# A scatter in front of all others, and VectorE's turned squares behind the choice of the group in front

## The chip, the cores and the metric

The kernel runs on one core of one Trainium2 chip. The metric is the device time of one execution in microseconds (us), the median of several; lower is better. The profile shows one further execution of the same program.

## The reference

The input x has 8 batches of 3584 rows of 192 values. First comes a causal convolution over the rows: 7 taps for each of 8 heads of 24 columns, the taps being a softmax of `weight`. Each of the 28672 rows that come out is then sent to one of 8 experts:

```
logits = x @ w_gate + modality_bias[modality_id]
e_idx  = argmax(logits, axis=1)
gate_w = softmax(logits)[e_idx]
out[rows of e] = gate_w * (relu(x[rows of e] @ w1[e]) @ w2[e])
```

w1[e] is 192 x 1024 and w2[e] is 1024 x 192.

## The kernel before, in words

**Routing.** The rows are taken in tiles of 120 positions of one batch; four tiles are a quad, and a group has 1, 1, 2, 1, 1, 2 and then 4 quads (`QUADS_OF_GROUP`). Groups are numbered from 0 here, so the words "groups two to six" of the change mean numbers 1 to 5 (the code gives pins to numbers 1 to 4). For each group:

- SP (SyncE) loads the rows `x` (L317, L320), one load per quad.
- `convolve` (L336) multiplies them on PE (TensorE) by a band matrix (`cv`, L365 while a group has its x whole, else L349); ACT (ScalarE) or DVE (VectorE) copies the result to one of four buffers `y` (L368, L370).
- `turn` (L381) lets DVE transpose squares of 32 x 32 of `y` into `turned` (L385); `gate` (L399) multiplies them on PE by w_gate (`gt`, L405); `logits` (L410) turns the result back and adds the bias (`lt` L412, `lg` L415).
- `choose` (L419) finds the expert on DVE: `top`, `ex`, `rk`, `first`, `oh` (L441, a one where the expert is), `den`.
- `place` (L453) counts on PE how many rows go to each expert (`rp`, L463, L466) and makes on DVE the row number of each token (`carry`, `pos`, `row`, `idx` L487).
- `send` (L492) lets POOL (GpSimd) scatter each tile's rows to the DRAM buffer `routed_rows`, one indirect DMA per tile (`scatter`, L249, issued on L251). Before a group's scatters POOL writes the token numbers into `y` (L448).

**Experts.** Groups 0 to 3 (5 quads, 20 tiles) are chunk 0. `table` (L626) shares the rows of a chunk out to slots, each of one expert. A `Slot` (L725) loads the expert's weights by SP (`raw1` L736, L738; `raw2` L741) and `bring` (L745) loads the routed rows (L771). The first slot's rows go to `raw2` of the other buffer and are turned by PE (`tps`, L802 to L804); `first` (L828) and `second` (L845) are then the two products of the expert (`hps` L835, `po` L855 and L859), which run for the rest of the kernel, with the routing of the later groups between them.

**What sets the order.** Each engine works off its own list in order. A scheduler orders the lists while the program is built, by its own estimate of when each instruction is ready; `tc.issue_after(i)` puts an instruction behind `i` in that order. SP's list is a queue as well: while its first instruction waits, all behind it wait. The load of the first slot's rows waits until all 20 scatters of chunk 0 have landed:

```
for c, name in scatters if self.i < always else ():
    if c <= chunk:
        tc.add_manual_dep(ld, name, ...)
```

Group 7's x stands in a buffer of four loads, one per quad. A convolution product takes the x of eight tiles, so that the first products of group 7 want the first two of these loads.

Of the kernel before, what the change touches and what calls it, by code (L numbers as in the profile page):

```python
# [9 lines left out]
F32 = mybir.dt.float32  # L10
F32R = mybir.dt.float32r
BF16 = mybir.dt.bfloat16
I32 = mybir.dt.int32
AF = mybir.ActivationFunctionType
ALU = mybir.AluOpType
# [3 lines left out]
P = 128  # L19
# [30 lines left out]
def conv_then_routed_ffn(ctx, tc, x, weight, modality, w_gate, mod_bias, w1, w2, out):  # L50
    nc = tc.nc
    NB, S, D = x.shape
# [11 lines left out]
    OVER = 2  # L64
    Q = 32
    NK = D // Q
    W = D + OVER
# [9 lines left out]
    const = ctx.enter_context(tc.tile_pool(name="const", bufs=1))  # L77
# [11 lines left out]
    turns, state = {}, {}  # L89

    def ring(pool, n, shape, dtype, name, tag=None):

        tag = tag or name
        k = turns[tag] = turns.get(tag, -1) + 1
        return pool.tile(shape, dtype, name=name, tag=f"{tag}_{k % n}", bufs=1)
# [20 lines left out]
    ident = const.tile([P, P], F32, name="ident")  # L116
# [4 lines left out]
    def warm(n):  # L121

        for _ in range(n):
# [7 lines left out]
        out=tri, in_=ones, compare_op=ALU.is_gt, fill=0.0, base=0,  # L131
        pattern=[[1, MB]], channel_multiplier=-1,
# [6 lines left out]
                   base=0, channel_multiplier=0, allow_small_or_imprecise_dtypes=True)  # L139
# [59 lines left out]
    def make_modality():  # L199
        both = const.tile([MB, 2, E], F32, name="both")  # L200
        nc.scalar.dma_start(out=both.rearrange("p m e -> p (m e)"),
                            in_=mod_bias.rearrange("m e -> (m e)").partition_broadcast(MB))
        step = const.tile([MB, E], F32, name="step")
        nc.vector.tensor_tensor(out=step, in0=both[:, 1, :], in1=both[:, 0, :], op=ALU.subtract)
        room, ids, each = modality_rows
        low = room[0:each, 4 * MB:6 * MB].rearrange("p (q s) -> p q s", q=2)
        with tc.issue_after(state["line"]):
            nc.vector.tensor_copy(out=low, in_=ids.rearrange("p q (s two) -> p q s two", two=2)[:, :, ::-1, 0])
        mt_ps = ring(ps_t, 4, [MB, 2, each], F32, "mt_ps", "t")
        for q in range(2):  # L210
            nc.tensor.transpose(out=mt_ps[:, q], in_=low[:, q, :], identity=ident[0:each, 0:each])
        mt = const.tile([MB, NB, NSB], F32, name="mt")
        with tc.issue_after(state["wg"]):
            nc.vector.tensor_copy(out=mt.rearrange("p b s -> p (b s)"), in_=mt_ps.rearrange("p q r -> p (q r)"))
        return both[:, 0, :], step, mt
# [43 lines left out]
    def routed(chunk, ins):  # L259
# [3 lines left out]
        tc.add_to_no_dep_group(f"rows{chunk}", ins)  # L263
        scatters.append((chunk, ins.name))

    def make_bias(dst, n, ids):
        nb = ids.shape[1]
        nc.gpsimd.tensor_tensor(
            out=dst.rearrange("p (s b) e -> p s b e", s=n), in0=ids.rearrange("p b s -> p s b").unsqueeze(3).broadcast_to([MB, n, nb, E]),
            in1=step.unsqueeze(1).unsqueeze(1).broadcast_to([MB, n, nb, E]), op=ALU.mult)  # L270
        nc.gpsimd.tensor_tensor(out=dst, in0=dst, in1=start_row.unsqueeze(1).broadcast_to([MB, n * nb, E]), op=ALU.add)
# [5 lines left out]
    class Group:  # L277
# [103 lines left out]
        def turn(self, q):  # L381

            t0 = self.b0 + 4 * q % NB
            self.turned = ring(gp, 2, [P, NK, 4, Q], F32, "turned")
            nc.vector.transpose(out=self.turned.rearrange("p k t c -> p t k c"),  # L385
                                in_=self.ys[4 * q // NB][:, t0:t0 + 4, OVER:W].rearrange("p t (k c) -> p t k c", c=Q))

        def part_turned(self, q):

# [29 lines left out]
        def choose(self):  # L419

            n = self.tiles
            lg = self.lg

            def per_tile(ap):
                return ap.unsqueeze(2).broadcast_to([MB, n, E])

            top = rt.tile([MB, NT], F32, name="top")[:, 0:n]
            nc.vector.tensor_reduce(out=top, in_=lg, axis=AX.X, op=ALU.max)
            ex = rt.tile([MB, NT, E], F32, name="ex", bufs=1)[:, 0:n]
            nc.vector.tensor_tensor(out=ex, in0=lg, in1=per_tile(top), op=ALU.subtract)  # L430
            self.oh_and_none = rt.tile([MB, NT, E], BF16, name="oh")[:, 0:n + (self.g < SUMMED)]
            self.oh = self.oh_and_none[:, 0:n]
            if self.g < SUMMED:
                nc.vector.memset(self.oh_and_none[:, n], 0.0)
            rk = rt.tile([MB, NT, E], F32, name="rk", bufs=1)[:, 0:n]
            nc.vector.scalar_tensor_tensor(out=rk, in0=ex, scalar=0.0, in1=ramp.unsqueeze(1).broadcast_to([MB, n, E]),
                                           op0=ALU.is_equal, op1=ALU.mult)
            state["exp"] = nc.scalar.activation(out=lg, in_=ex, func=AF.Exp).ins
            first = rt.tile([MB, NT], F32, name="first")[:, 0:n]
            nc.vector.tensor_reduce(out=first, in_=rk, axis=AX.X, op=ALU.max)  # L440
            nc.vector.tensor_tensor(out=self.oh, in0=rk, in1=per_tile(first), op=ALU.is_equal)  # L441
            den = rt.tile([MB, NT], F32, name="den")[:, 0:n]
            nc.vector.tensor_reduce(out=den, in_=lg, axis=AX.X, op=ALU.add)
            nc.vector.tensor_scalar(out=den, in0=den, scalar1=1e-9, scalar2=None, op0=ALU.add)
            for i, y in enumerate(self.ys):
                nc.vector.reciprocal(out=y[0:MB, self.b0:self.b0 + self.nb, 0], in_=den[:, i * self.nb:(i + 1) * self.nb])
                with tc.issue_after(state["scatter"]) if "scatter" in state else nullcontext():
                    nc.gpsimd.iota(y.bitcast(I32)[0:MB, self.b0:self.b0 + self.nb, 1], pattern=[[S, self.nb]],  # L448
                                   base=self.b0 * S + (self.block + i) * MB - CUT + MB - 1,
                                   channel_multiplier=-1)  # L450
# [47 lines left out]
    FIRST = GROUPS_OF_CHUNK[0]  # L498
# [54 lines left out]
    def load_early(g):  # L553
        early.append(Group(g, chunk_of[g]))
        for q in range(early[-1].quads):
            early[-1].load(q, g >= CLEARED)
# [339 lines left out]
    for g in range(CLEARED):  # L896
        with tc.issue_after(state["band"]) if g >= BEFORE_BAND else nullcontext():
            load_early(g)
    start_row, step, mt = make_modality()
    init_tables()  # L900
    make_keep()
    first_bias = const.tile([MB, 6 * NB, E], F32, name="first_bias")
    make_bias(first_bias, 6, mt[:, :, 0:6])
    for y in y_bufs[1:]:
        clear(y)
# [176 lines left out]
```

## Time and profile before

| | us |
|---|---|
| median of 3 executions | 1239.13 (1236.37, 1239.13, 1240.28) |
| the profiled execution | 1235.66 |
| span of its instructions | 1233.9 |
| PE busy in it | 1212.0 (98%) |
| DVE busy | 964.4 (78%) |
| ACT busy | 721.0 (58%) |
| POOL busy | 526.6 (43%) |

The span runs from the first to the last instruction; 1.8 us of the execution lie around it. PE busy nearly all the time says that an end is moved only by what makes PE wait, by what PE has to do and by its clock. The waits lie in the first 65 us, where the routing of chunk 0 runs before the first expert can start; so the rows further down are nearly all from that stretch. Times in them are us from the start of the span.

### The profile page before, as it was taken

To read this page: it belongs to the slowest core of one execution; us is meant where nothing else is said; L and a number is where in the kernel's file an instruction comes from. 1 tells how busy PE (TensorE), PEld (TensorE's weight loads), DVE (VectorE), ACT (ScalarE), POOL (GpSimd) and SP (SyncE) were. 2 spreads that over 40 slices of the span, in tenths; PEclk is the share of its full clock that TensorE was granted. 3 is DMA by queue.
4 is the path that set the end of the run, shared out by engine and by line. 5 is a ranking of instruction groups with operands and counts; after the bars stand their busy time and mean duration, and the time that the engine had idled before them with its cause. 6 is when DMAs were issued, how large, how long until landed. Compare 5 with 4: busy or idle time off the path is not lost.

```text
span 1233.9 us, 28026 instructions
## 1 busy us (share of the span) xinstructions
PE 1212.0 (98%) x9244; PEld 1198.9 (97%) x9244; DVE 964.4 (78%) x2453; ACT 721.0 (58%) x1584; POOL 526.6 (43%) x549
## 2 busy tenths in 40 slices
PE   9899999999999999999999999999999999999996
PEld 7899999999999999999999999999999999999995
DVE  7787786888788888888878887777766766787894
ACT  2365565565666556666655665555555555566783
POOL 7756564636344343545435344344352122112221
PEclk9999999999999999999999999999999999999998
DMA  8897563345544354345432554233262344953271
GB/s 217 235 239 182 126 175 78 76 107 150 137 87 114 77 130 109 66 113 147 126 70 59 109 124 123 53 73 61 62 169 56 81 106 91 255 125 96 43 190 38
DMA packets 308448, 144.29 MB, mean 117 GB/s; under 512 B 222922, under 2 KB 294930, under 8 KB 308293
## 3 DMA queue, kind: packets, MB, share of 16 engines
q1 hardware_dynamic: 284574, 97.83, 36.8%
q0 software_dynamic: 22752, 44.54, 11.6%
q8 instruction: 74, 1.21, 0.4%
q14 instruction: 81, 0.66, 0.2%
q10 hardware_dynamic: 967, 0.03, 0.0%
HBM read 116.58 MB, written 51.82 MB: 136 GB/s over the span
## 4 chain that ended last, share of the span: by engine, by line
PE 85%; DVE 5%; DMA 4%; issue 2%; ACT 1%; POOL 1%; SPq 1%; POOLq 0%; DVEq 0%; ACTq 0%
PE hps L835 39%; PE po L855 25%; PE po L859 12%; PE gt L405 4%; PE cv L349 3%; PE cv L365 2%; DMA raw<-in_moe_w_dram 1%; DVE hl L839 1%; DMA xr<-in_x_dram 1%; DVE w1b L110 1%; DVE xl L110 1%; DMA routed_rows<-y,idx 1%; DVE w2b L110 1%; DMA near<-routed_rows 1%; ACT lowp L871 1%
## 5 line engine op out<-in xcount | busy, mean ns | idle before, releaser
L855 PE MATMUL po<-w2b,hh 128*128 128x384 f32 x1824 | 555.9, 355 | 0.0
L835 PE MATMUL hps<-sxh,w1b 128*128 128x256 f32 x1824 | 481.8, 287 | 3.1 <-DVE hl L839 1.7
L839 DVE SCALAR_TENSOR_TENSOR hl<-hps,hh 128x512 fp32r<-128x512 f32 x456 | 311.6, 685 | 198.0 <-ACT hh L838 195.6
L838 ACT ACTIVATE hh<-hps 128x512 fp32r<-128x512 f32 x456 | 272.8, 598 | 327.7 <-PE hps L835 322.2
L859 PE MATMUL po<-w2b,hl 128*128 128x192 f32 x1824 | 443.0, 253 | 0.0
L874 POOL DMA_INDIRECT out_dram<-o,tags x228 | 236.3, 1036 | 382.0 <-DVE o L873 323.3
L251 POOL DMA_INDIRECT routed_rows<-y,idx x240 | 260.8, 1087 | 304.1 <-DVE hl L839 145.7
L835 PE MATMUL hps<-sxs,w1b 128*128 128x256 f32 x1824 | 363.2, 281 | 0.4 <-DVE sxs L822 0.4
L835 PEld LDWEIGHTS hps<-sxh,w1b 128*128 128x128 f32 x1824 | 344.5, 189 | 8.4 <-DVE hl L839 7.8
L859 PEld LDWEIGHTS po<-w2b,hl 128*128 128x128 f32 x1824 | 345.7, 190 | 0.0
L855 PEld LDWEIGHTS po<-w2b,hh 128*128 128x128 f32 x1824 | 344.1, 189 | 0.5 <-DVE o L873 0.2
L835 PEld LDWEIGHTS hps<-sxs,w1b 128*128 128x128 f32 x1824 | 279.8, 189 | 0.7 <-issue 0.7
L835 PE MATMUL hps<-sxl,w1b 128*128 128x256 f32 x912 | 256.0, 281 | 0.0
L835 PEld LDWEIGHTS hps<-sxl,w1b 128*128 128x128 f32 x912 | 172.8, 189 | 0.0
L110 DVE TENSOR_TENSOR w1b<-raw,w1b 128x512 fp32r<-128x512 f32 x152 | 101.4, 675 | 5.9 <-ACT w1b L108 5.5
L871 ACT ACTIVATE lowp<-po,tags 128x192 f32<-128x192 f32 x228 | 83.6, 417 | 31.1 <-PE po L855 29.7
L108 ACT CAST w1b<-raw 128x512 fp32r<-128x512 f32 x152 | 92.7, 620 | 2.0 <-DMA raw<-in_moe_w_dram 1.3
L110 DVE TENSOR_TENSOR w2b<-raw,w2b 128x384 fp32r<-128x384 f32 x152 | 80.7, 541 | 8.2 <-ACT w2b L108 7.8
L873 DVE SCALAR_TENSOR_TENSOR o<-po,tags,lowp 128x192 f32<-128x192 f32 x228 | 84.6, 411 | 2.2 <-ACT lowp L871 2.2
L820 ACT CAST sxs<-tp 64x128 fp32r<-64x128 f32 x224 | 66.7, 298 | 30.7 <-DVE tp L795 28.0
L108 ACT CAST w2b<-raw 128x384 fp32r<-128x384 f32 x152 | 75.9, 512 | 1.0
L822 DVE TENSOR_TENSOR sxs<-tp,sxs 64x128 fp32r<-64x128 f32 x224 | 64.8, 289 | 8.6
(158 smaller groups left out, 962.8 us busy)
## 6 DMA issues: line engine op xcount, KB each, us to landing
raw<-in_moe_w_dram SPq DMA_DIRECT2D x38, 768.0 KB
raw<-in_moe_w_dram SPq DMA_DIRECT2D x38, 512.0 KB
raw<-in_moe_w_dram SPq DMA_DIRECT2D x76, 256.0 KB
near<-routed_rows SPq DMA_DIRECT2D x208, 64.0 KB
xr<-in_x_dram SPq DMA_DIRECT2D x32, 384.0 KB
x<-in_x_dram SPq DMA_DIRECT2D x26, 384.0 KB
routed_rows<-filler SPq DMA_DIRECT2D x9, 776.0 KB
far<-routed_rows SPq DMA_DIRECT2D x208, 32.0 KB
```

Source lines behind the costliest of these rows:

```text
L108: nc.scalar.copy(out=hi, in_=raw)
L110: return nc.vector.tensor_tensor(out=lo, in0=raw, in1=f(hi), op=ALU.subtract).ins
L251: state["scatter"] = nc.gpsimd.indirect_dma_start(out=scr, out_offset=bass.IndirectOffsetOnAxis(ap=idx, axis=0), in_=src, in_offset=None,).ins
L820: nc.scalar.copy(out=hi, in_=raw)
L835: nc.tensor.matmul(hps[:, u, :], wa[:, c, fs], mv[z], start=n == 0, stop=n == len(terms) - 1)
L838: nc.scalar.activation(out=hh, in_=hps, func=AF.Relu)
L839: hl_ins = nc.vector.scalar_tensor_tensor(out=hl, in0=hps, scalar=0.0, in1=f(hh), op0=ALU.max, op1=ALU.subtract)
L855: nc.tensor.matmul(po, hh[:, u, js], wb[:, c, :], start=c == 0, stop=c == NF - 1, skip_group_check=True)
L859: nc.tensor.matmul(po[:, 0:D], hl[:, u, js], wb[:, c, 0:D], start=False, stop=False, skip_group_check=True)
L871: nc.scalar.activation(out=lowp, in_=po[:, D:2 * D], func=AF.Copy, scale=gate)
L873: turn_behind(nc.vector.scalar_tensor_tensor(out=o, in0=po[:, 0:D], scalar=gate, in1=lowp, op0=ALU.mult, op1=ALU.add))
L874: st = nc.gpsimd.indirect_dma_start(out=out, out_offset=bass.IndirectOffsetOnAxis(ap=tag.bitcast(I32)[:, j, 1:2], axis=0), in_=o, in_offse ...
```

## The change

Three edits. (1) A new function `scatter_once` issues, after the bands and the gate are made, one indirect DMA of 128 rows of two values from `ident` into a DRAM buffer of its own, `first_rows`, which nobody reads. (2) `choose` keeps its `oh` instruction in `state["oh"]`. (3) In `turn`, for groups 1 to 4 the first quad's transposition is put behind the `oh` of the group in front, and the second quad's (only group 2 has one) behind the `idx` of the group in front. Pins are of order alone and add no wait.

```diff
+    def scatter_once():
+        at = const.tile([P, 1], I32, name="at")
+        nc.gpsimd.iota(at, pattern=[[0, 1]], base=0, channel_multiplier=1)
+        first = nc.dram_tensor("first_rows", (P, OVER), F32, kind="Internal").ap()
+        nc.gpsimd.indirect_dma_start(out=first, out_offset=bass.IndirectOffsetOnAxis(ap=at, axis=0),
+                                     in_=ident[:, 0:OVER], in_offset=None)
...
             self.turned = ring(gp, 2, [P, NK, 4, Q], F32, "turned")
-            nc.vector.transpose(out=self.turned.rearrange("p k t c -> p t k c"),
-                                in_=self.ys[4 * q // NB][:, t0:t0 + 4, OVER:W].rearrange("p t (k c) -> p t k c", c=Q))
+            pin = state["idx" if q else "oh"] if 0 < self.g <= FIRST else None
+            with tc.issue_after(pin) if pin else nullcontext():
+                nc.vector.transpose(out=self.turned.rearrange("p k t c -> p t k c"),
+                                    in_=self.ys[4 * q // NB][:, t0:t0 + 4, OVER:W].rearrange("p t (k c) -> p t k c", c=Q))
...
-            nc.vector.tensor_tensor(out=self.oh, in0=rk, in1=per_tile(first), op=ALU.is_equal)
+            state["oh"] = nc.vector.tensor_tensor(out=self.oh, in0=rk, in1=per_tile(first), op=ALU.is_equal).ins
...
             load_early(g)
+    scatter_once()
     start_row, step, mt = make_modality()
```

The scheduler then orders other instructions anew as well. After the first expert products of slot 0 the lists of all engines are again the same; before them they differ in places. The line numbers of the changed kernel are 7 to 10 higher.

**VectorE, from the copy of group 0's convolution to its `idx` (L487, in the changed kernel L496).** `y_182` is the buffer of groups 0 and 1. Before:

```order
L385 STREAM_TRANSPOSE turned<-y_182 128x4x6x32
L370 COPY y_182<-cv 120x2x4x24
L412 STREAM_TRANSPOSE lt<-gt 128x128
L415 TENSOR_TENSOR lg<-lt,first_bias 120x32
L428 TENSOR_REDUCE top<-lg 120x4
L385 STREAM_TRANSPOSE turned<-y_182 128x4x6x32
L430 TENSOR_TENSOR ex<-lg,top 120x32
L436 SCALAR_TENSOR_TENSOR rk<-ex,ramp 120x32
L440 TENSOR_REDUCE first<-rk 120x4
L443 TENSOR_REDUCE den<-lg 120x4
L441 TENSOR_TENSOR oh<-rk,first 120x32
```

Now:

```order
L421 STREAM_TRANSPOSE lt<-gt 128x128
L424 TENSOR_TENSOR lg<-lt,first_bias 120x32
L437 TENSOR_REDUCE top<-lg 120x4
L439 TENSOR_TENSOR ex<-lg,top 120x32
L445 SCALAR_TENSOR_TENSOR rk<-ex,ramp 120x32
L449 TENSOR_REDUCE first<-rk 120x4
L452 TENSOR_REDUCE den<-lg 120x4
L450 TENSOR_TENSOR oh<-rk,first 120x32
L394 STREAM_TRANSPOSE turned<-y_182 128x4x6x32
L453 TENSOR_SCALAR den<-den 120x4
L477 TENSOR_TENSOR carry<-rp,carry_175 120x8
```

Group 1's transposition, which stood inside group 0's choice, stands right behind its `oh`.

**SP, from the last x load of group 6 to the first slot's rows and beyond.** `x_767` (in the changed kernel `x_770`) is the x of group 7, `raw1_0` and `raw2_0` the first slot's weights, `raw2_1<-routed_rows` the first slot's rows. Before:

```order
L320 DMA x_767<-in_x_dram 128x4x192 x2
L731 TENSOR_LOAD tab_595
...
L741 DMA raw2_0_87<-in_moe_w2_dram 128x8x192
...
L771 DMA raw2_1_88<-routed_rows 128x2x194
L771 ISA
L771 DMA raw2_1_88<-routed_rows 128x2x194
L771 ISA
L771 DMA tags_639<-routed_rows 128x4x2
L320 DMA x_767<-in_x_dram 128x4x192 x2
```

Now:

```order
L327 DMA x_770<-in_x_dram 128x4x192
L740 TENSOR_LOAD tab_598
...
L750 DMA raw2_0_87<-in_moe_w2_dram 128x8x192
...
L780 DMA raw2_1_88<-routed_rows 128x2x194
L780 ISA
L780 DMA raw2_1_88<-routed_rows 128x2x194
L780 ISA
L780 DMA tags_642<-routed_rows 128x4x2
L327 DMA x_770<-in_x_dram 128x4x192 x3
```

One of the two loads of group 7's x that stood in front of the table has moved behind the first slot's rows and tags.

**PE, from the gate products of group 6 to the first slot's turned rows, in the changed kernel, with what each waits for.** `DMAHW7` is the semaphore that the first two loads of `x_770` raise.

```order
L414 MATMUL gt_859<-turned_837,wg_whole_215 128x128 x5
L372 MATMUL cv_1115<-x_770,band_202 120x192 [waits DMAHW7_49,DVE_49]
L372 MATMUL cv_1115<-x_770,band_202 120x192
L414 MATMUL gt_871<-turned_857,wg_whole_215 128x128 [waits DVE_49]
L414 MATMUL gt_871<-turned_857,wg_whole_215 128x128 x5
L414 MATMUL gt_881<-turned_869,wg_whole_215 128x128 [waits DVE_49,Activation_49]
L414 MATMUL gt_881<-turned_869,wg_whole_215 128x128 x5
L811 MATMUL tps_909<-ident_95,raw2_1_88 128x128 [waits DMASW2_49,DMAHW4_49,DMASW1_49,DMASW0_49]
```

This piece has the same instructions in the same places in both kernels; what is new is that the second load that `cv_1115` wants is one that SP issues behind the first slot's rows.

## Rows read from the trace of the kernel before

**Rows 1.** The page: its first line, and busy time by engine.

```profile
span 1233.9 us, 28026 instructions
PE 1212.0 (98%) x9244; PEld 1198.9 (97%) x9244; DVE 964.4 (78%) x2453; ACT 721.0 (58%) x1584; POOL 526.6 (43%) x549
```

**Rows 2.** Windows: length, busy time of PE, PEld, DVE, ACT, POOL, PE clock, DMA share.

```profile
400.00:700.00 300.00, 299.11 (x2281) 297.41 (x2281) 244.79 (x593) 183.02 (x407) 137.70 (x138) 1.00 0.45 103
```

**Rows 3.** Timeline of POOL: start, duration, engine, line, [idle time before].

```profile
11.63 0.92 POOL L268 TENSOR_TENSOR first_bias<-mt,step 120x384 f32<-120x384 f32 x1 [1.62 <-DVE mt L214]
...
14.07 1.00 POOL L271 TENSOR_TENSOR first_bias<-first_bias,both 120x384 f32<-120x384 f32 x1
...
21.56 1.10 POOL L251 DMA_INDIRECT routed_rows<-y,idx  x1 [3.13 <-ACT lg L438]
...
32.43 1.01 POOL L251 DMA_INDIRECT routed_rows<-y,idx  x1 [0.31 <-POOL y L448]
...
46.91 0.99 POOL L251 DMA_INDIRECT routed_rows<-y,idx  x1 [0.31 <-issue]
```

**Rows 4.** Timeline of DVE, group 0's choice and place, and group 2's `idx`.

```profile
16.70 0.19 DVE L415 TENSOR_TENSOR lg<-lt,first_bias 120x32 f32<-120x32 f32 x1
...
17.03 0.98 DVE L385 STREAM_TRANSPOSE turned<-y 128x768 f32<-128x768 f32 x1
17.93 0.15 DVE L430 TENSOR_TENSOR ex<-lg,top 120x32 f32<-120x32 f32 x1
...
18.73 0.19 DVE L441 TENSOR_TENSOR oh<-rk,first 120x32 bf16<-120x32 f32 x1
...
19.42 0.17 DVE L468 TENSOR_TENSOR carry<-rp,carry 120x8 f32<-120x8 f32 x1 [0.20 <-PE rp L466]
...
20.20 0.32 DVE L412 STREAM_TRANSPOSE lt<-gt 128x128 f32<-128x128 f32 x1
20.44 0.13 DVE L487 CAST idx<-row 120x4 int32<-120x4 f32 x1
...
31.30 0.15 DVE L487 CAST idx<-row 120x8 int32<-120x8 f32 x1
```

**Rows 5.** Timeline of PE, from the stall at 35 us to the first slot's turned rows.

```profile
36.75 0.18 PE L463 MATMUL rp<-oh,tri 120*120 120x40 bf16 x1 [1.87 <-DVE oh L441]
...
37.73 4.57 PE L405 MATMUL gt<-turned,wg_whole 128*128 128x128 f32 x24 [0.60 <-DVE den L444]
...
49.31 2.94 PE L405 MATMUL gt<-turned,wg_whole 128*128 128x128 f32 x24 [1.14 <-ACT y L368]
52.09 0.81 PE L365 MATMUL cv<-x,band 128*120 128x192 f32 x4
52.74 2.84 PE L405 MATMUL gt<-turned,wg_whole 128*128 128x128 f32 x24
55.42 0.38 PE L802 MATMUL tps<-ident,raw 128*128 128x128 f32 x2
```

**Rows 6.** Windows as in rows 2, of the stretch in which the clock fell.

```profile
39.00:40.00 1.00, 1.00 (x6) 1.00 (x6) 0.19 (x1) 0.00 (x0) 0.93 (x1) 0.50 1.28 343
```

**Rows 7.** Timeline of SP's queue, the loads from 50 to 53 us.

```profile
50.11 0.97 SPq L771 DMA_DIRECT2D raw<-routed_rows x2
51.28 0.37 SPq L771 DMA_DIRECT2D tags<-routed_rows x1
51.70 1.06 SPq L320 DMA_DIRECT2D x<-in_x_dram x2
```

**Rows 8.** Waits of SP's queue, 36 to 60 us: who for whom, sum, times, longest.

```profile
SPq L771 <- DMA routed_rows<-y,idx: 8.2, 4, 7.1
```

**Rows 9.** DMA queues, SP's own from 50 us to 56.2 and to 57.4: packets, MB.

```profile
q1 hardware_dynamic: 1734, 0.90, 65.3%
...
q1 hardware_dynamic: 2070, 1.23, 69.6%
```

**Rows 10.** The chain that ended last, in order of time: an x load early on.

```profile
12.52 4.30 DMA x<-in_x_dram
```

## The prediction, made before the changed kernel ran

> **What bounds the kernel now.** I read the page first. PE is busy for 1212.0 of 1233.9 us [rows 1]; in the windows over the span, the 300 us from 400 on have 299.11 us of PE work at full clock [rows 2]. So whatever moves the moment at which the first expert starts moves the end by as much, unless something late takes it back, and there is hardly an idle microsecond late that could. I therefore read the first 65 us engine by engine.
>
> PE's timeline [rows 5] has two stalls there: 1.87 and 0.60 us before 37.73, and 1.14 us before 49.31. After the first, the clock was 0.50, that is 1.2 GHz in place of 2.4 [rows 6], and the 24 gate products took 4.57 us where the next 24 took 2.94. From 49.31 PE has no gap until the first slot's turned rows at 55.42, which is the point that I follow: I call it the start of the experts. In that piece stand the gate products of group 6, then the first product pair of group 7's convolution (52.09), then gate products again (52.74), then the turned rows.
>
> POOL's timeline [rows 3]: from 21.56 on scatter follows scatter, each 0.99 us with 0.31 before it; the last of chunk 0 starts at 46.91 and is over at 47.90. SP's queue [rows 7] issues the first slot's rows at 50.11, and the waits of that queue say why: its longest, 7.1 us, is for scatters [rows 8]. So from the last scatter's end to the rows' issue are 50.11 - 47.90 = 2.21 us, which is the landing. Behind the rows and the tags SP issues x at 51.70. In the kernel before nothing of this stands on PE's path: the two x loads that PE needs at 52.09 stand in SP's list in front of the first slot's weights.
>
> **The scatter of its own.** It adds one POOL instruction, and one iota (the iotas nearby are short). On the one side it may cost POOL time: before `first_bias` POOL was idle for 1.62 us [rows 3], from 10.01 to 11.63; a first scatter with its issue takes 0.31 + 1.10 us by the nearest rows, and at worst the 0.68 us named below on top, 2.1 in all. That pushes `first_bias` by at most 0.5 us, to an end of 15.6 instead of 15.07, and DVE reads it at 16.70 [rows 4]. Hidden, and 1.1 us would be left; if that cover were gone, the choice of group 0 would start later by the excess.
>
> On the other side it may take the first-use cost out of the first real scatter. That scatter's index was done at 20.57 [rows 4] and it started at 21.56, 0.99 us later, where scatters in the stream start 0.31 after what they follow; and it took 1.10 in place of 0.99 [rows 3]. So 0.68 + 0.11 = 0.79 us are special to it. Nothing of the trace shows whether this is the price of being the first or of something else, a wake-up after the wait, say; the bounds are 0 and 0.79. I take 0.79, since the 0.31 of the other scatters is the nearest row to a scatter that is not the first.
>
> **The pins.** Inside group 0's choice DVE ran group 1's transposition (17.03, 0.98 us), so `ex` came at 17.93 [rows 4]. Pinned behind `oh` it lets `ex` come at about 17.13 and `oh` 0.80 earlier, and then fills the 0.20 us that DVE waited for PE before `carry`. Of what stood in front of `idx`, that wait and the 0.24 us that `lt` took from 20.20 on go; the transposition itself still stands there. So `idx` comes some 0.45 us earlier. For group 2 the same move is needed: its first scatter stood at 32.43 with its index ready at 31.45 [rows 3, 4], and a stream that runs 1.2 us earlier would otherwise wait for it.
>
> First scatter: 0.45 + 0.68 = 1.13 us earlier at its start, 1.24 at its end (bounds 0.45 and 1.5). The last of chunk 0 then ends at 47.90 - 1.24 = 46.66, and SP can issue the first slot's rows at 46.66 + 2.21 = 48.87.
>
> **What is now late.** The order of SP's list puts the second load of group 7's x behind the rows and tags. PE's list still has group 7's first product pair in front of the last gate products of group 6 and of the turned rows, and it now waits for that load. So this load is issued at 48.87 + (51.70 - 50.11) = 50.46, and PE reaches the pair at about 51 (52.09, or up to 1.2 earlier).
>
> How long the load takes: by the nearest row, an early x load of the same 384 KB, 4.30 us from the end of its issue [rows 10], so with its issue some 4.7. That load did not stand behind 512 tags of 8 bytes. For the same place in the queue I count bytes: from 50 us on SP's queue has to move rows (0.40 MB), tags (0.004), one x load (0.39) and the second (0.39). By 56.2 it had moved 0.90 MB and by 57.4 1.23 [rows 9], so that the first x load's bytes were through at about 55.8 and the second's at about 57.3. A load has landed when its last engine is done, and the two loads run into each other; I take the later time, 5.6 us after the issue at 51.70, and keep 4.1 (the first load's bytes alone) and 6.5 (0.9 more for what may come after the last byte) for the range. The pair then starts at 50.46 + 5.6 = 56.1 in place of 52.09. The order of the work behind it stays: 55.42 - 52.09 = 3.33 us later the experts start, at 59.4. That is 59.4 - 55.42 = 4.0 us late.
>
> **The clock.** PE would be idle for some 5 us. After a stall of 1.87 + 0.60 us the clock was at 0.50 and 24 products cost 4.57 - 2.94 = 1.63 us more [rows 5, 6]. The stretch behind the new stall has the same 24 products; I take 1.6 us, with bounds 0 and 2.5 (if the work is at half clock for half as long again). The old stall at 35 us may shrink or stay, which no longer matters: PE waits for the load in any case.
>
> **Sum.** 4.0 + 1.6 = 5.6 us later, of which the scatters' 1.24 us are already taken off. On the profiled execution's 1235.66 us that gives 1241.3. That execution is 3.5 us below the median of the three runs, 1239.13; the four together have a mean of 1237.9, and I predict from there, rounding, 1243.5. A measurement of this kernel tells about 0.3%, 3.7 us, from no change.
>
> A rule speaks for a shorter stall: by the Trainium skill (DMA: Bandwidth & Descriptors, section Anatomy of one DMA) a transfer takes about 2.0 us plus its bytes over 436 GB/s, an estimate of 2.9 us for 384 KB; by that the pair would start at 53.4 and the sum be 1.3 us without the clock. The trace doesn't agree, since the load of rows 10 took 4.30 us and the bytes of rows 9 needed longer still; the sum goes by these.
>
> **The rivals.** *The load is early enough (0.24).* The x load lands soon after its issue, so the stall is short and the scatters' 1.24 us nearly pay for it. For it: a DMA share of 0.45 over the long run, and only light traffic on the queues at 49 us. Against it: the tags in front and the scatters beside. At 4.1 us the pair starts at 54.6, 2.5 us late, and with an unharmed clock the experts start 2.5 us late: no change that can be measured, 1240.4. It decides at a landing of 5.3 us with the clock unharmed, or 3.7 with it harmed: under that the kernel isn't slower. The skill's estimate above, 1.3 us or 1239.2, is a case of this rival.
>
> *The head's gain counts in full (0.05).* If PE's list did not wait (the pair moved, or the load was there by 51), the experts would start 1.24 us earlier and the stall at 35 us could go with its clock, 1.87 + 0.60 + 1.63: up to 5.3 us in all, 1233. The order of the lists speaks against it: the load would have to be issued by 47, and the rows in front of it wait for a scatter that ends at 46.66 at best.
>
> *The scatter of its own saves nothing (0.08).* Then only 0.45 us come off in place of 1.24, and the sum is 6.4: 1244.3. What speaks for it is that 0.99 us are also what a wake-up after a wait could cost.
>
> **How the numbers follow.** The forecast has 0.63. Slower by over 0.3%: the forecast and the third rival, 0.71, less 0.03 for forecasts whose 4.0 us without a loss of clock end within 0.3% by the runs' spread: 0.68. Faster: the second rival, 0.05. The rest, 0.27, is no change. The forecast's own range is from 4.0 (clock unharmed) to 5.6 + 0.9 + 0.9 = 7.4 us more (load and clock at their upper bounds): 1241.9 to 1245.3. The whole range goes down to the first rival, 1240.4, and up to the third on top of the forecast's upper end, 0.8 us more, 1246.1; on both sides I add the 1.2 us by which mean and median of the shown runs differ: 1239.2 to 1247.3.
>
> **What would show it.** In the changed kernel's profile: the first scatter starting near 20.4 with 0.99 us; the transposition right behind `oh`; the first slot's rows issued near 48.9 and one x load more behind them; PE's `cv` of group 7 with some 5 us of idle time before it that a DMA of x ended; a clock of 0.50 in the stretch after it; the turned rows near 61 and not 55.4. From there on the same work as before. The prediction is wrong if that idle time is under 2 us, if the rows are issued later than before, or if the experts start as late as forecast and the end does not move with them.

## The result, and the profile after

| | before | changed |
|---|---|---|
| median of 5 executions each, us | 1238.46 (1236.37 to 1240.28) | 1250.92 (1250.09 to 1252.0) |
| the profiled execution, us | 1235.66 | 1252.0 |
| the first slot's turned rows, us from the span's start | 55.42 | 71.14 |

The ratio is 1.0106, with a 95% interval of 1.0095 to 1.0117: slower by 12.5 us. The forecast was 1243.5, its range ended at 1247.3.

The page of the changed kernel, the lines of [rows 1]:

```profile
span 1250.3 us, 28026 instructions
PE 1219.0 (97%) x9244; PEld 1204.9 (96%) x9244; DVE 966.4 (77%) x2453; ACT 721.0 (58%) x1584; POOL 529.0 (42%) x551
```

PE is busy 7 us longer for the same products, which is the clock, and the span is 16.4 us longer. That is more than 12.5 because the profiled execution of before is 2.8 us under its median and the changed one 1.1 us over. The experts start 71.14 - 55.42 = 15.7 us later, so the loss is again in the head. POOL's timeline there, against [rows 3]:

```profile
10.35 1.08 POOL L270 DMA_INDIRECT first_rows<-ident,at  x1 [0.19 <-issue]
...
12.03 0.91 POOL L275 TENSOR_TENSOR first_bias<-mt,step 120x384 f32<-120x384 f32 x1 [0.60 <-DVE mt L214]
...
25.50 1.06 POOL L251 DMA_INDIRECT routed_rows<-y,idx  x1 [6.62 <-DVE idx L496]
...
38.03 1.00 POOL L251 DMA_INDIRECT routed_rows<-y,idx  x1 [1.53 <-DVE idx L496]
...
52.51 0.99 POOL L251 DMA_INDIRECT routed_rows<-y,idx  x1 [0.30 <-issue]
```

On POOL the new scatter is as cheap as foreseen: the bias starts 0.40 us later. But the first routed scatter comes 3.94 us later, and the last of chunk 0 5.6 us later, as POOL now also waits 1.53 us for group 2's index. PE's timeline, against [rows 5], says what it stood behind:

```profile
20.28 2.89 PE L372 MATMUL cv<-x,band 128*120 128x192 f32 x8 [3.15 <-DMA x<-in_x_dram]
...
65.29 1.61 PE L372 MATMUL cv<-x,band 128*120 128x192 f32 x4 [4.92 <-DMA x<-in_x_dram]
66.69 4.61 PE L414 MATMUL gt<-turned,wg_whole 128*128 128x128 f32 x24
71.14 0.38 PE L811 MATMUL tps<-ident,raw 128*128 128x128 f32 x2
```

The second stall is the one that the prediction is about. The first, 3.15 us for the x of group 2, was nowhere in it. It delays the counts of group 0, which stand behind those products on PE, as DVE's timeline shows (against [rows 4]):

```profile
23.61 0.17 DVE L477 TENSOR_TENSOR carry<-rp,carry 120x8 f32<-120x8 f32 x1 [3.71 <-PE rp L475]
...
24.42 0.17 DVE L496 CAST idx<-row 120x4 int32<-120x4 f32 x1
```

SP's queue, against [rows 7]:

```profile
12.59 6.51 SPq L327 DMA_DIRECT2D x<-in_x_dram  x6
...
58.22 0.97 SPq L780 DMA_DIRECT2D raw<-routed_rows  x2
59.38 0.37 SPq L780 DMA_DIRECT2D tags<-routed_rows  x1
59.80 1.77 SPq L327 DMA_DIRECT2D x<-in_x_dram  x3
```

The first slot's rows are issued 8.1 us later: 5.6 of it is the last scatter, and 2.5 is the landing, 58.22 - 53.50 = 4.72 us in place of 2.21. The six early x loads take 6.51 us to issue. What they moved from 13 to 17 us, SP's queue in the changed kernel (packets, MB, share of the 16 engines' time):

```profile
q1 hardware_dynamic: 298, 0.23, 51.0%
```

and in the kernel before:

```profile
q1 hardware_dynamic: 1471, 1.10, 94.7%
```

So half the engines' time went on packets, but only a fifth of the bytes came through. The windows behind both stalls (columns as in rows 2) have the clock at 0.50, the lower of its two levels:

```profile
20.00:25.00 5.00, 4.72 (x18) 4.66 (x19) 0.89 (x7) 0.96 (x2) 0.00 (x0) 0.50 1.11 327
67.00:70.00 3.00, 3.00 (x16) 3.00 (x16) 0.47 (x2) 0.00 (x0) 2.38 (x4) 0.50 1.07 336
```

### The profile page after: what moved, and what is told of

It is laid out like the page before. It is cut to its first block, busy times and chain, and to the rows that moved or that the text cites. A ratio compares the mean times of both kernels' runs of the same rounds, so it can differ in the third digit from the quotient of the medians.

```text
span 1250.3 us, 28026 instructions
## 1 busy us (share of the span) xinstructions
PE 1219.0 (97%) x9244; PEld 1204.9 (96%) x9244; DVE 966.4 (77%) x2453; ACT 721.0 (58%) x1584; POOL 529.0 (42%) x551
## 4 chain that ended last, share of the span: by engine, by line
PE 84%; DVE 6%; DMA 3%; issue 2%; ACT 2%; SPq 1%; POOL 0%; DVEq 0%; POOLq 0%
PE hps L844 38%; PE po L864 24%; PE po L868 12%; PE gt L414 4%; PE cv L356 3%; PE cv L372 3%; DVE hl L848 1%; DMA x<-in_x_dram 1%; DVE w1b L110 1%; DMA raw<-in_moe_w_dram 1%; ACT lowp L880 1%; DMA near<-routed_rows 1%; DVE sxs L831 0%; SPq L780 0%; DVE xl L110 0%
```

## The experiments

Theory A: the loss has two causes that add, the bytes that the new scatter writes and the place of one x load. Theory B: it all comes from the new order of the lists. The runs fell on several chips. On some of them the kernel before takes 1272 to 1274 us, as their PE idles in the head for another reason (below), so a time is compared only with the kernel before on the same chip:

| run | us | before beside it | ratio | 95% interval |
|---|---|---|---|---|
| scatter_only | 1242.98 | 1238.14 | 1.0042 | 1.0026 to 1.0058 |
| pins_only | 1245.88 | 1238.14 | 1.0066 | 1.0050 to 1.0082 |
| x_behind | 1243.56 | 1238.14 | 1.0045 | 1.0027 to 1.0063 |
| pins_x8 | 1238.06 | 1238.14 | 1.0000 | 0.9990 to 1.0010 |
| pitch | 1237.53 | 1237.57 | 0.9997 | 0.9983 to 1.0010 |
| after_wide | 1244.63 | 1237.57 | 1.0051 | 1.0037 to 1.0065 |
| after_x8 | 1242.99 | 1237.57 | 1.0039 | 1.0025 to 1.0053 |
| after_wide_x8 | 1237.83 | 1237.57 | 1.0003 | 0.9991 to 1.0015 |
| wide | 1272.93 | 1273.90 | 0.9987 | 0.9965 to 1.0010 |
| twice | 1279.50 | 1273.90 | 1.0043 | 1.0024 to 1.0063 |
| plain | 1272.27 | 1273.90 | 0.9998 | 0.9978 to 1.0017 |
| early | 1273.46 | 1273.90 | 0.9997 | 0.9981 to 1.0014 |
| pins_w2 | 1270.26 | 1272.13 | 0.9986 | 0.9969 to 1.0003 |
| pins_again | 1270.67 | 1272.13 | 0.9985 | 0.9973 to 0.9997 |
| pin_first | 1268.44 | 1272.13 | 0.9970 | 0.9955 to 0.9985 |
| before_again | 1273.87 | 1272.13 | 1.0017 | 1.0003 to 1.0032 |
| pins_w2_again | 1269.89 | 1273.46 | 0.9975 | 0.9959 to 0.9992 |
| pin_first_again | 1269.01 | 1273.46 | 0.9957 | 0.9939 to 0.9975 |

### The two edits apart

**scatter_only**: the first edit alone, no pins. Only POOL's list changes.

```diff
+    scatter_once()
     start_row, step, mt = make_modality()
```

(The function is that of the change.)

> The scatter of its own alone, no pins; SP's, PE's, VectorE's and ACT's lists stay those of the kernel before. Theory A (the scatter's own writes hold up the x loads beside it): in the changed kernel's trace PE waited 3.15 us for group 2's x at 17 us and the index of group 0 came 4.0 us later; here the same stall of some 3 us before the first products of group 2, the first routed scatter near 25 and not 21.56, and, since the last scatter of chunk 0 ends the wait for the first slot's rows, the experts 4 to 6 us later: 1242 to 1245 us. Theory B (all of the loss comes from the new order of the lists, that is from the pins): x as early as before, no stall at 17 us, 1238 to 1239 us, or 0.8 less if the first scatter's special cost goes.

The timeline of several engines:

```profile
11.97 7.36 SPq L327 DMA_DIRECT2D x<-in_x_dram  x6
...
20.64 2.64 PE L372 MATMUL cv<-x,band 128*120 128x192 f32 x8 [3.95 <-DMA x<-in_x_dram]
...
25.77 0.13 DVE L494 CAST idx<-row 120x4 int32<-120x4 f32 x1
26.82 1.06 POOL L251 DMA_INDIRECT routed_rows<-y,idx  x1 [7.85 <-ACT lg L445]
```

As theory A has it: the lists of SP, PE and DVE are those of before, and still x is late and PE stalls for 3.95 us. The last two rows settle another point: with a scatter in front, the first routed one still starts 26.82 - 25.90 = 0.92 us after its index, where it was 0.99, and takes 1.06 us, where it was 1.10. It saves 0.1 us, not 0.79.

**pins_only**: the pins alone, that is the change without its first edit:

```diff
-    scatter_once()
     start_row, step, mt = make_modality()
```

> The pins alone, no scatter of its own. Theory A: no stall at 17 us, the index of group 0 some 0.4 us earlier than before (20.2 and not 20.57), but PE's stall of about 5 us before group 7's first products, with half clock behind it: 4 to 6 us more than before, 1242.5 to 1244.5. Theory B: the whole loss is here, 1249 to 1252, the stall at 17 us included.

```profile
34.51 0.15 DVE L470 TENSOR_TENSOR carry<-rp,carry 120x8 f32<-120x8 f32 x1
...
40.20 0.37 SPq L738 DMA_DIRECT2D raw<-in_moe_w_dram  x1
...
46.73 1.00 POOL L251 DMA_INDIRECT routed_rows<-y,idx  x1 [0.30 <-issue]
...
52.46 0.97 SPq L773 DMA_DIRECT2D raw<-routed_rows  x2
54.05 2.01 SPq L320 DMA_DIRECT2D x<-in_x_dram  x3
...
59.97 1.60 PE L365 MATMUL cv<-x,band 128*120 128x192 f32 x4 [5.36 <-DMA x<-in_x_dram]
```

The stall for x is there, and none stands at 17 us, but the cost, 7.7 us, is above the 4 to 6 expected. The last scatter is 0.18 us earlier than in [rows 3], yet the rows are issued 2.35 us later than in [rows 7]. The first two of these rows in the kernel before:

```profile
32.60 0.17 DVE L468 TENSOR_TENSOR carry<-rp,carry 120x8 f32<-120x8 f32 x1 [0.47 <-PE rp L466]
...
38.11 0.37 SPq L736 DMA_DIRECT2D raw<-in_moe_w_dram  x1
```

The pins make the counts of group 3, the last of chunk 0, 1.91 us later, with each group's transposition now behind the choice in front on DVE. The table needs those counts, and the weights need the table: 2.09 us later. That their bytes then stand in front of the last scatter's and hold up its landing is a guess (theory W below).

**x_behind**: the kernel before with the one load moved. The pin's edit:

```diff
-            pin = "load" if self.g == KEPT + 2 else "x"
+            pin = "load" if self.g == KEPT + 2 or self.g == KEPT + 1 and q > 0 else "x"
```

> The kernel before with one load moved: group 7's second x load stands behind the first slot's rows and tags on SP, as in the changed kernel; PE's, VectorE's, ACT's and POOL's lists are untouched. This measures the step that the prediction called what is now late, by itself. The prediction's own numbers: load issued at 51.7, landed 5.6 later, the pair at 57.3 in place of 52.09, then 1.6 for the clock: 5.2 + 1.6 = 6.8 us more, 1245 us. Rival (the order of that load costs little, most is from elsewhere): under 3 us more, below 1241.5.

```profile
50.26 0.97 SPq L771 DMA_DIRECT2D raw<-routed_rows  x2
51.84 1.68 SPq L320 DMA_DIRECT2D x<-in_x_dram  x3
...
57.86 1.60 PE L365 MATMUL cv<-x,band 128*120 128x192 f32 x4 [5.50 <-DMA x<-in_x_dram]
...
63.82 0.38 PE L802 MATMUL tps<-ident,raw 128*128 128x128 f32 x2
```

The load alone costs 5.4 us, under the 6.8 expected and over the 3 of the rival. The pair starts 6.0 us after the first of those loads is issued (forecast 5.6), and the turned rows 5.96 us after the pair, where it was 3.33 in [rows 5] and the forecast had 3.33 + 1.6. Both terms are larger than forecast and the cost is smaller, which fits [rows 5] being an early profile: the turned rows here are 8.4 us behind its 55.42, but 6.3 behind those of `pitch` below, which has the SP and PE lists of before.

**pins_x8**: the pins, and group 7's first two x loads as one that stands in front of the weights:

```diff
+                if self.g == KEPT + 1 and q == 1:
+                    self.xr.append(xr)
+                    return
+                both = 4 if self.g == KEPT + 1 and q == 0 else 0
+                to = self.x[:, 0:8, :] if both else xr
-                ld = nc.sync.dma_start(out=xr, in_=x[b0:b0 + 4, s0 - HALO:s0 + MB, :].rearrange("b s d -> s b d"))
+                ld = nc.sync.dma_start(out=to, in_=x[b0:b0 + 4 + both, s0 - HALO:s0 + MB, :].rearrange("b s d -> s b d"))
```

> The pins alone, and group 7's first two x loads made one load of eight tiles, which stands in front of the first slot's weights; all other lists as with the pins alone. If the load behind the rows is what the pins cost (A): the stall before group 7's first products is gone and the time is 1236 to 1239, that is no loss against the kernel before and perhaps 1 to 3 us of gain, as the head's stall at 35 us may shrink. If the pins cost otherwise (B: the order of PE and VectorE), 1244 or more stays.

```profile
52.14 0.97 SPq L778 DMA_DIRECT2D raw<-routed_rows  x2
...
53.70 0.91 PE L370 MATMUL cv<-x,band 128*120 128x192 f32 x4
...
57.34 0.38 PE L809 MATMUL tps<-ident,raw 128*128 128x128 f32 x2
```

No idle time stands before the pair, and the whole loss of the pins is gone, though the rows are as late as with the pins alone. Late rows cost only where PE waits for the load behind them: 5.4 us for the load and 2.35 for the rows make 7.75, where 7.7 was measured.

### What the scatter does to the loads beside it

**wide**: `scatter_only` with rows of 128 values:

```diff
-        first = nc.dram_tensor("first_rows", (P, OVER), F32, kind="Internal").ap()
+        first = nc.dram_tensor("first_rows", (P, P), F32, kind="Internal").ap()
...
-                                     in_=ident[:, 0:OVER], in_offset=None)
+                                     in_=ident, in_offset=None)
```

> The scatter of its own alone, with rows of 128 values (512 bytes) in place of two (8 bytes). Seen so far: behind the scatter of its own SP's six x loads took 7.36 us to issue and not 3.64, and the DMA engines moved under 100 GB/s from 13 to 17 us; but in the kernel before a dip of the same kind, from 350 to 140 to 250 GB/s, stands at 23.0 to 25.5 us, right behind the first routed scatter, and it is gone from there once the other scatter came in front (four x loads issued in 2.15 us and not 4.08). Theory S (writes of 8 bytes are what holds the others up): with 512 bytes the stall of 3.95 us before group 2's products is gone or under 1 us, and the time is that of the kernel before. Theory F (the program's first scatter, whatever it writes, holds up the transfers behind it for 2.5 to 4 us): the six x loads still take over 6 us to issue, the stall stays at 3 to 4 us, and the time is 1242 to 1244.

```profile
12.10 3.60 SPq L327 DMA_DIRECT2D x<-in_x_dram  x6
...
20.86 0.13 DVE L494 CAST idx<-row 120x4 int32<-120x4 f32 x1
...
21.89 1.06 POOL L251 DMA_INDIRECT routed_rows<-y,idx  x1 [3.02 <-ACT lg L445]
```

64 times the bytes, and no hold: theory F (the first scatter, whatever it writes) falls, S (small writes) stands. The first routed scatter again starts 0.90 us after its index. The dip behind it, which the expectation names, did not go with a scatter in front: four x loads still take 3.22 us here and 3.17 in `pitch`. In all runs they took 3.1 us or more where SP issued them at most 5.1 us behind the 776 KB that it writes into `routed_rows` (`filler`), and 2.2 or less where it was 5.7 or more.

**twice**: two scatters of 8-byte rows.

```diff
+        for n in range(2):
+            first = nc.dram_tensor(f"first_rows{n}", (P, OVER), F32, kind="Internal").ap()
```

> Two such scatters of 8-byte rows behind one another, each to a buffer of its own, no pins. Theory S (every small scatter holds the others up): the hold doubles, the stall before group 2's products is 6 to 8 us and the time 1246 or more. Theory F (only the first does): the stall is 3 to 4.5 us as with one, and the time 1242 to 1245, the second costing POOL some 1.3 us in front of the bias, which has about 1.1 us of room left.

```profile
12.33 8.13 SPq L328 DMA_DIRECT2D x<-in_x_dram  x6
...
21.51 2.88 PE L373 MATMUL cv<-x,band 128*120 128x192 f32 x8 [4.59 <-DMA x<-in_x_dram]
```

The hold did not double: 4.59 us in place of 3.95, on another chip. By itself this would speak for F, which `wide` rules out. The trace shows an overlap: half of the 32 packets of the two small writes are out by 12.9 us, the other half go between 14.0 and 18.4 us, inside the hold, and from 18 us on the engines move 338 GB/s again.

**plain**: the same 1 KB by a plain DMA that POOL issues at 12.77 us. The call is also pinned behind one of POOL's clearings of `y`; of the edit only the DMA is shown.

```diff
+        nc.gpsimd.dma_start(out=first, in_=ident[:, 0:OVER])
```

> The same 128 writes of 8 bytes to the same kind of buffer by a plain DMA that POOL issues, without an index, some 2 us later on POOL's list; no pins. If the bytes or their size hold up the x loads (S), or any DMA of POOL's queue does, the dip stands behind it as well, some 2 us later, and PE waits 2 us or more for x. If it takes an indirect one, the first of the program (F): no dip there, no stall, 1238 us, and the dip behind the first routed scatter at 23 us is back.

Its windows from 17 to 21 us, and those of `wide` behind them (last two columns: DMA share, GB/s):

```profile
17.00:21.00 4.00, 3.87 (x30) 3.73 (x31) 3.58 (x17) 1.14 (x4) 2.06 (x7) 1.00 1.24 157
```

```profile
17.00:21.00 4.00, 3.76 (x29) 3.50 (x30) 3.55 (x18) 1.26 (x4) 1.84 (x6) 1.00 1.10 326
```

The hold is there without any scatter, some 4 us later than with one: 157 GB/s in place of 326. So are the packets of the write, at 15.9 to 16.3 us and not at 12.0 to 12.6 as in `scatter_only`. The wait of PE that S expected does not come, as the loads that PE needs at 17 us have landed by then. So it is the write, not the instruction.

**early**: `scatter_only` with the call ahead of the modality loads.

```diff
+    scatter_once()
     modality_rows = load_modality()
```

> The scatter of its own put ahead of the modality loads at about 2 us, no pins. Theory F: the hold of 2.5 to 4 us falls between 3 and 8 us, where the DMA engines move little; the x loads from 12 us on issue in about 3.6 us, PE has no stall at 17 us, and the four x loads at 21.5 us issue in about 2.1 us as the dip there is gone; the time is that of the kernel before within 2 us, 1236 to 1240, or it is later by what the held loads of the taps and the bands cost, up to 3 us. Theory S or any theory by which the scatter spoils something that lasts: the stall before group 2's products stays at 3 us or more.

```profile
13.94 3.59 SPq L328 DMA_DIRECT2D x<-in_x_dram  x6
```

No hold on the x loads, ratio 0.9997, though they begin some 1.8 us later than in `wide`. Nothing lasting is spoilt; it is a matter of what runs in the few us behind the write. The time alone would not say so: on this chip a first routed scatter that comes 2.6 us later than in `wide` (24.48 us, not 21.89) doesn't show in it either.

**pitch**: `scatter_only` with the index 64 times as far apart, so that the rows of 8 bytes lie 512 bytes apart:

```diff
-        nc.gpsimd.iota(at, pattern=[[0, 1]], base=0, channel_multiplier=1)
-        first = nc.dram_tensor("first_rows", (P, OVER), F32, kind="Internal").ap()
+        nc.gpsimd.iota(at, pattern=[[0, 1]], base=0, channel_multiplier=64)
+        first = nc.dram_tensor("first_rows", (64 * P, OVER), F32, kind="Internal").ap()
```

> The scatter of its own alone with rows of 8 bytes again, but 512 bytes apart in the buffer in place of one behind the other. Seen: 8 bytes side by side hold up the x loads (six issued in 7.36 us), 512 bytes side by side do not (3.60). Theory N (writes that lie near one another, many in a few hundred bytes, are what holds the others up): here no hold, six x loads in some 3.6 us, no stall before group 2's products. Theory Z (any write of 8 bytes does, wherever it lies): six x loads in 6 us or more and a stall of 3 us or more.

```profile
11.77 3.82 SPq L327 DMA_DIRECT2D x<-in_x_dram  x6
...
49.82 4.57 PE L412 MATMUL gt<-turned,wg_whole 128*128 128x128 f32 x24 [1.19 <-ACT y L375]
...
57.56 0.38 PE L809 MATMUL tps<-ident,raw 128*128 128x128 f32 x2
```

No hold and no loss: theory N. Of the two pitches run, 8 bytes and 512, only writes side by side cost the others something. The other rows are a check on the profile of before: with the SP and PE lists of before and its time, the experts start here at 57.56 us, so the 55.42 of [rows 5] was an early one by some 2 us. Most of that is the clock: 24 gate products take 4.57 us here where they took 2.94 in [rows 5].

### The changed kernel with one cause undone, and both

**after_wide** is the changed kernel with the diff of `wide`, **after_x8** with that of `pins_x8`, **after_wide_x8** with both.

> The changed kernel with one thing undone: the scatter of its own writes rows of 512 bytes. All lists are those of the changed kernel. If the bytes of that scatter and the place of one x load are the two causes (A), this gives back the scatter's part, some 4 to 7 us of the 12.5: a ratio to the kernel before of about 1.005 to 1.007, no stall at 17 us, the stall of some 5 us before group 7's products still there. If the changed kernel loses through something else (C), 1.009 or more stays.

```profile
11.80 3.62 SPq L327 DMA_DIRECT2D x<-in_x_dram  x6
...
58.33 1.61 PE L372 MATMUL cv<-x,band 128*120 128x192 f32 x4 [4.69 <-DMA x<-in_x_dram]
```

> The changed kernel with the other thing undone: group 7's first two x loads are one load in front of the first slot's weights. If A: the stall before group 7's products is gone, the stall at 17 us stays, and the ratio to the kernel before is that of the scatter alone, about 1.004 to 1.006. If C: 1.009 or more.

```profile
20.26 2.89 PE L377 MATMUL cv<-x,band 128*120 128x192 f32 x8 [3.68 <-DMA x<-in_x_dram]
...
58.93 0.91 PE L377 MATMUL cv<-x,band 128*120 128x192 f32 x4
```

> The changed kernel with both undone, so that what is left of the change is a scatter in front of the others and the order of VectorE's list. If A: no difference from the kernel before that can be measured, ratio 0.998 to 1.002. If the change has a gain of its own that the two losses covered (the first scatter's 0.79 us and the stall at 35 us with its clock): 0.997 or less. If C: over 1.004.

```profile
57.63 0.38 PE L816 MATMUL tps<-ident,raw 128*128 128x128 f32 x2
```

Each takes out its own stall and leaves the other: 7.1 us remain without the small rows, 5.4 without the late load, together 12.5, which is the loss of the changed kernel (each of the two has an interval of 1.7 us to either side). With both undone no loss and no gain can be measured, though the rest of the new lists is there. This settles theory A against B.

### What stayed open

**pins_w2** is `pins_only` with the largest weight load behind the rows and tags, and **pins_again** is its neighbour:

```diff
             self.load_second = load_second
-            load_second()
+            if i:
+                load_second()
...
             state["load"] = ld
+            if first:
+                self.load_second()
```

**pin_first** keeps the pin of group 1 alone:

```diff
-            pin = state["idx" if q else "oh"] if 0 < self.g <= FIRST else None
+            pin = state["idx" if q else "oh"] if self.g == 1 else None
```

**before_again** is the kernel before; **pins_w2_again** and **pin_first_again** repeat two of them.

> The pins alone, with the first slot's last weight load (w2, 786 KB) moved behind its rows and tags on SP; all other lists as with the pins alone. Theory W (the last scatter lands late because the weights are in front of it in the DMA queues): from the last scatter's end to the rows' issue 2 to 3 us in place of 4.7, the rows at 49.7 to 50.7 and not 52.46. The x load behind them now has w2 in front of it, so that the stall before group 7's products may end no earlier, and the time can be anything from 2 us less to 1 us more than with the pins alone. Theory V (the rows are late for another reason, the order of PE or VectorE): still 4 us or more from the last scatter's end to the rows' issue.

> The pins alone once more, as the neighbour of the run above: rows some 2 us later than before, a stall of some 5 us before group 7's products, a ratio of 1.005 to 1.008 to the kernel before.

> Only the pin of group 1's transposition behind group 0's choice; SP's list is that of the kernel before. By the prediction's step: the index of group 0 some 0.45 us earlier and so the last scatter; a gain of at most that, which is no difference that can be measured, 0.998 to 1.002. If the pin itself harms (a later table, later weights): 1.003 or more.

> The kernel before once more, for a second profile: if the first profile's experts' start at 55.42 us was an early one, this one is 1 to 3 us later, with a span nearer the median less 1.8; otherwise within 0.5 us of 55.42.

> The pins alone with w2 behind the first slot's rows and tags, once more. Where the head runs as in the first profile of the kernel before (last scatter of chunk 0 ends near 47.9): by W 2 to 3 us from that end to the rows' issue, rows at 49.5 to 50.7; by V 4 us or more. The time: 1242 to 1247, since the x load that PE waits for has w2 in front of it now.

> Only the pin of group 1's transposition, once more. If the 0.3% that it gained on the other chip is the pin's: 0.996 to 0.998. If it is the other chip's stalls that it happened to dodge: 0.999 to 1.002 here.

All six fell on chips where the kernel before takes 1272 us and more. PE's timeline of `before_again`:

```profile
74.00 1.64 PE L365 MATMUL cv<-x,band 128*120 128x192 f32 x4 [6.81 <-issue]
...
78.79 0.38 PE L802 MATMUL tps<-ident,raw 128*128 128x128 f32 x2
```

There PE idles where it waits for nothing that the profile shows, 6.81 us in this row, and the experts start 23.4 us later than in [rows 5]. So the expectations that give times in us do not apply, and `pitch`, not `before_again`, answers whether 55.42 was early. Under that idling, the pins cost nothing (`pins_again`, 0.9985), as the x load is early enough beside it. Here `pins_again` missed its 1.005 to 1.008. From the last scatter's end to the rows' issue there were 4.75 us in `pins_again` (53.38 to 58.13) and 3.91 in `pins_w2` (53.21 to 57.12), 3.53 in its repeat: in the direction of theory W, but neither the 2 to 3 us that it expected nor the 4 or more of the rival. So that the weights hold up the last scatter's landing is argued, not shown. That the pins lengthen it is shown: on chips of the first kind it took 4.5 to 4.7 us in all six profiles with the pins, and 2.0 to 3.1 us in the four without them. `pin_first` came out 0.3 and 0.4% faster than the kernel before on two such chips, where the same kernel against itself (`before_again`) was off by 0.17%; it had been expected to gain nothing that can be measured. It wasn't run on a chip of the first kind, so whether it beats the kernel before there is open too.

## Why the prediction was wrong

**The direction and the named stall were right.** The load behind the rows, PE's wait of some 5 us (4.92), the clock of 0.50 behind it, the same work from there on: all stand in the changed kernel's trace. By itself this part cost 5.4 us (`x_behind`), where the prediction's terms make 6.8 and the sum, with 1.24 us taken off for the scatters, 5.6. But one of the prediction's own signs of being wrong came true as well: the rows were issued later than before, at 58.22 and not 50.11 us.

**"The scatter of its own" is the step that failed.** It said "Hidden, and 1.1 us would be left", from POOL's timeline alone, and for POOL that was right. The transfer that the instruction sets off was not costed: its 1 KB held the x loads of SP's queue for some 4 us, the x of group 2 came too late, PE stalled, the clock fell, and the counts of group 0 with all scatters came 4 us later and more. That is 4.8 us alone (`scatter_only`) and 1250.92 - 1238.46 less the 7.1 of `after_wide`, 5.4, within the change. It is this term that took the time out of the range: without the scatter it is 1245.88 (`pins_only`), with wide rows 1244.63 (`after_wide`), and the range ended at 1247.3. No rival named it either: that the scatter saves nothing was there, that it harms a neighbour was not.

**"I take 0.79" for the first-use cost was wrong too**; 0.1 us is what a scatter in front saved (`scatter_only`). The third rival, by which it saves nothing, describes that better, with its 0.8 us; whether the 0.9 us from index to scatter are a wake-up, no run shows.

**"The pins" had the wrong sign at their end.** The index of group 0 came earlier, 0.17 us by `pins_only` and not 0.45 (one profile each, and such profiles differ by 0.4 us: 20.57 us before, 20.95 in `x_behind`), but only this end was followed. The counts of group 3 came 1.91 us later, and the table and the weights with them. So "SP can issue the first slot's rows at 46.66 + 2.21 = 48.87" became 52.46 with the pins alone. The 2.21 us, "which is the landing", were taken as fixed, and were 4.72 in the changed kernel.

**"What is now late"** was right in size: 5.6 us for the load, 5.5 measured in the changed kernel from the issue of the first of the loads behind the tags (59.80 to 65.29), and 4.9 to 6.0 over the four runs that have this stall on chips of the first kind. The estimate of 2.9 us by the Trainium skill (DMA: Bandwidth & Descriptors, section Anatomy of one DMA) stayed far below all of them; that section fits its formula to transfers that GpSimd issues, and SP issues these. **"The clock"** was in the main too small: 1.6 us forecast, 71.14 - 65.29 - 3.33 = 2.5 in the changed kernel and 1.5 to 2.6 over the same four runs, as the pair itself runs at half clock as well (1.61 for 0.81) and the clock comes back at different times.

**The sum.** Forecast 5.6. Measured: the load 5.4, the later rows 2.3, the held x loads 4.8 to 5.4, together 12.5 to 13.1 where the change cost 12.5.

## What to carry to other kernels

A DMA that is added to warm something up can harm the transfers of other queues: look at what is in flight behind it (here up to 18 us, for a scatter that POOL issued at 10.35), not only at the idle time of the engine that issues it. Where a scratch write is needed, rows of 512 bytes, or small rows 512 bytes apart, did no harm here. And when a pin makes one thing earlier, follow what it makes later to the last consumer of the stage, here the counts, the table and the weights, and look at the list of every queue for a load that has changed sides of a wait.

## What was not expected of the hardware

128 writes of 8 bytes side by side in DRAM cut what the loads beside them moved from 1.10 MB to 0.23 MB in 4 us, while the same 128 writes 512 bytes apart, or 64 times the bytes in rows of 512, left the loads their pace (six issued in 3.82 and 3.60 us, not 7.36). It does not take a scatter. The 16 packets of the small write took at most 0.03 us each, while a packet of the loads beside them took up to 4.1 us (`scatter_only`; 0.7 in `wide`, both from 13 to 18 us). The Trainium skill (DMA: Bandwidth & Descriptors, section Why small descriptors are slow) gives small descriptors (the single pieces that a transfer is cut into) a price of their own at HBM, some 3 cycles a packet and 32 bytes of metadata an operation; by that the harm would lie in the small transfer itself. The runs show it in its neighbours. Which part of the memory or of the DMA engines it is, no run here shows.
